# Fused two-stream attention block: interleaved layer norm, scaled copies out of PSUM, a new order of v products and weight loads, and sixteen matmuls on zeros

## The chip, the cores and the metric

The kernel runs on one core of one Trainium2 chip. A core has five engines that run their own instruction queues and meet through semaphores: PE (TensorE, matrix products, with weight loads that the profile counts apart as PEld), DVE (VectorE), ACT (ScalarE), POOL (GpSimd) and SP (SyncE, used here to issue DMAs). The metric is the device time of one execution in microseconds, lower is better. Three executions of the kernel before took 125.85, 125.17 and 124.64 us; the median is 125.17 us.

## The reference

There are two token streams, image (B = 2, 256 tokens each) and text (2 x 32 tokens), of width D = 1152, all in bfloat16. Each is normalized, scaled and shifted by rows that depend on a conditioning vector `c`, projected to q, k, v with its own weights; attention runs over the 288 joined tokens; the result goes through an output projection, is gated and added to the input.

```python
mod_i = (_silu(c) @ wmod_img).reshape(B, 6, 1, D)     # shi, sci, gai = rows 0, 1, 2
mod_t = (_silu(c) @ wmod_txt).reshape(B, 6, 1, D)     # sht, sct, gat = rows 0, 1, 2
hi = _layernorm(x_img) * (1 + sci) + shi
ht = _layernorm(x_txt) * (1 + sct) + sht
qkvi = hi @ wqkv_img
qkvt = ht @ wqkv_txt
...
scores = jnp.einsum('bqd,bkd->bqk', q, k) * D ** (-0.5)
a = jnp.einsum('bqk,bkd->bqd', softmax(scores), v)
out_i = x_img + gai * (ai @ wo_img)
out_t = x_txt + gat * (at @ wo_txt)
```

## The kernel before, in words

The order of each engine's work is the order in which the program is written (`manual_schedule`, line 62); no planner moves anything. Each engine has one ordered list of instructions; a wait stands in that list, with what follows it behind.

**Tiles.** The 512 image tokens are four tiles of 128 tokens (0 and 1 of batch 0, 2 and 3 of batch 1). The width is nine blocks of 128 (index `kt`), in four chunks of 2, 2, 2 and 3 blocks (`KC`, line 49). Normalized tokens `xn_i` are transposed on PE into `hT_i`, block by block, with the width on the partitions. Scale and shift are applied to `hT_i` after the transposes, as a factor and an addend for each partition (`apply_mod`, line 181: engine code 0 is DVE, 1 is POOL, 2 is ACT).

**Loads.** All weights are loaded by SP in one order. At the start: tiles 0 and 1 of x, then the first chunks of the scale weights `w_sc_i` and of the v weights `w_v_i`, then tiles 2 and 3 of x, then the other three pairs of chunks (lines 94 to 100), x of the text, the shift weights `w_sh_i` and the q weights `w_q_i`. The full weight matrices live in a pool of six buffers (line 54), so the seventh and later loads (lines 315 to 324) wait until the last reader of an earlier one is done: they are, in order, the text shift and scale weights `w_sh_t` and `w_sc_t`, then `w_k_i`, `w_q_t`, `w_k_t`, `w_ga_i`, `w_v_t`, `w_o_i`, `w_ga_t`, `w_o_t`. The eleventh, `w_v_t`, takes the buffer of the fifth.

**Front part (lines 214 to 269).** `silu_c` transposes `c` on PE and computes silu on ACT and DVE. Then, for each tile: `ln_stats` (three `bn_stats`, one aggregate on DVE, a square root on ACT), `ln_apply` (a reciprocal and one `tensor_scalar` on DVE), `x_transposes` (nine PE transposes into two PSUM tiles, and two ACT copies of five and four blocks into `hT_i`). `mod_scale(ch)` makes the factors of one chunk from `w_sc_i` with 18 or 27 matmuls of two columns. `v_part(i, half, ch)` adds one chunk's products to the v of tile i, half a row of 512 columns; seven such accumulators stay in PSUM until the last chunk. The statements of the four tiles are interleaved by hand.

**Middle.** `v_rest` (columns 1024 to 1151 of v), the eighth v product (line 303), the shift factors (`mod_cols` of `w_sh_i`, line 308; copies on DVE and ACT, lines 309 and 310), the shift added to `hT_i`, and `mod_rows(w_v_i, 4)`, which makes the effect of the shift on v as a row. A row made by `mod_rows` reaches the tokens by way of DRAM: PE products, a copy out of PSUM, two small DMAs from POOL to the scratch `mod_scratch` (line 344), and DMAs from POOL that read it back spread over the partitions (lines 350, 392, 533).

**q and k (line 369).** `qk_img` runs 81 matmuls of 512 columns for q, then 81 for k: first three output blocks together, then six groups of one block, nine matmuls each. `hooks` are functions called ahead of the group with that index. In the q pass, `v_shift` (DVE adds) stands ahead of group 5 and `txt_rows_shift` ahead of group 6; `txt_rows_scale` follows the q pass and also issues the four read-backs `mb_t`. In the k pass, `txt_modulate` (two DVE operations on the text tokens `xn_t`, lines 400 and 401) stands ahead of group 5, and `txt_transposes` (nine PE transposes, one ACT copy to `hT_t`, lines 406 and 407) ahead of group 8. The q and k products of the text (line 418, 162 matmuls) come next and read `hT_t`.

**Rest.** Scores and softmax, the v of the text, attention (line 500), output projections (line 568) with gates, and the output DMAs.

Of the kernel before, what the change touches and what calls it, by code (L numbers as in the profile page):

```python
# [14 lines left out]
def kernel(  # L15
# [14 lines left out]
    nc = tc.nc  # L30
# [42 lines left out]
    def load_w(src, c0, ksplits=((0, KT),)):  # L73
        t = wpool.tile([P, KT, D], bf, tag="w")
        for (k0, k1) in ksplits:
            nc.sync.dma_start(t[:, k0:k1, :], w_view(src)[:, k0:k1, c0:c0 + D])
        return t
# [31 lines left out]
    make_identity(nc, ident[:])  # L109
    eps_t = const.tile([P, 1], f32)  # L110
    nc.vector.memset(eps_t[:], EPS)
    sT32 = const.tile([P, KT, 32], bf)
    nc.gpsimd.memset(sT32[:], 0.0)
    shT32 = const.tile([P, KT, 32], bf)
    nc.gpsimd.memset(shT32[:], 0.0)


    e18 = small.tile([P, B * KT], f32, bufs=1)
    sT = const.tile([P, KT, B], bf)

    def silu_c():
        cT_ps = ps_sm.tile([P, B * KT], bf, tag="sm")
        nc.tensor.transpose(cT_ps[:], c18[:], ident[0:B * KT, 0:B * KT])
        nc.scalar.activation(e18[:], cT_ps[:], ACT.Exp, scale=-1.0)
        nc.vector.tensor_scalar_add(e18[:], e18[:], 1.0)
        nc.vector.reciprocal(e18[:], e18[:])
        nc.vector.tensor_mul(sT[:], cT_ps[:].rearrange("p (b kt) -> p kt b", b=B),
                             e18[:].rearrange("p (b kt) -> p kt b", b=B))
        nc.gpsimd.tensor_copy(sT32[:, :, 0:B], sT[:])
# [3 lines left out]
    def evac(out_ap, in_ap):  # L133
        if evac_idx[0] % 2 == 0:
            nc.vector.tensor_copy(out_ap, in_ap)  # L135
        else:
            nc.scalar.copy(out_ap, in_ap)  # L137
        evac_idx[0] += 1

    def ln_stats(x_ap, np_):  # L140
        stats = small.tile([P, NCH, 6], f32, tag="stats")
        for k in range(NCH):
            nc.vector.bn_stats(stats[0:np_, k, :], x_ap[:, k * CH:(k + 1) * CH])  # L143
        mv = small.tile([P, 2], f32, tag="mv")
        nc.vector.bn_aggr(mv[0:np_, :], stats[0:np_, :, :])
        rstd = small.tile([P, 1], f32, tag="rstd")
        nc.scalar.activation(rstd[0:np_, :], mv[0:np_, 1:2], ACT.Sqrt, bias=eps_t[0:np_, :])
        return mv, rstd

    def ln_apply(x_ap, np_, out_ap, mv, rstd):  # L150
        nc.vector.reciprocal(rstd[0:np_, :], rstd[0:np_, :])
        nc.vector.tensor_scalar(out_ap, x_ap, mv[0:np_, 0:1], rstd[0:np_, :], op0=ALU.subtract, op1=ALU.mult)  # L152

    xn_i = act.tile([P, NIT, D], bf, tag="A")
    hT_i = act.tile([P, KT, B * NI], bf, tag="Bt")

    def x_transposes(i):
        for (k0, k1) in ((0, 5), (5, KT)):
            tp = ps_mm.tile([P, 5, P], bf, tag="mm")
            for kt in range(k0, k1):  # L160
                nc.tensor.transpose(tp[:, kt - k0, :], xn_i[:, i, kt * P:(kt + 1) * P], ident[:])  # L161
            nc.scalar.copy(hT_i[:, k0:k1, i * P:(i + 1) * P], tp[:, 0:k1 - k0, :])  # L162

    mod_i = const.tile([P, 2 * KT, B], f32, name="mod_img")

    def mod_cols(wt, out_ps, j0, j1):
        for j in range(j0, j1):
# [13 lines left out]
    def apply_mod(kt, t0, t1, shift, eng):  # L181
        b = t0 // TPB
        sl = hT_i[:, kt, t0 * P:t1 * P]
        ap = mod_i[:, kt, b:b + 1] if shift else mod_i[:, KT + kt, b:b + 1]
        op = ALU.add if shift else ALU.mult
        if eng == 0:
            nc.vector.tensor_scalar(sl, sl, ap, None, op0=op)  # L187
        elif eng == 1:
            if shift:
                nc.gpsimd.tensor_scalar(sl, sl, 1.0, ap, op0=ALU.mult, op1=ALU.add)  # L190
            else:
                nc.gpsimd.tensor_scalar(sl, sl, ap, 0.0, op0=ALU.mult, op1=ALU.add)  # L192
        elif shift:
            nc.scalar.activation(sl, sl, ACT.Identity, bias=ap, scale=1.0)
        else:
            nc.scalar.activation(sl, sl, ACT.Identity, scale=ap)
# [5 lines left out]
    def v_part(i, half, ch):  # L202
        k0, k1 = KC[ch]
        if ch == 0:
            vacc[i, half] = ps_mm.tile([P, VW], f32, tag="mm", name=f"va{i}{half}")
        ps = vacc[i, half]
        for kt in range(k0, k1):
            nc.tensor.matmul(ps[:], lhsT=hT_i[:, kt, i * P:(i + 1) * P], rhs=w_v_i[:, kt, half * VW:(half + 1) * VW],  # L208
                             start=(kt == 0), stop=(kt == KT - 1))
        if k1 == KT:  # L210
            evac(v_i[:, i, half * VW:(half + 1) * VW], ps[:])


    silu_c()
    st = ln_stats(x_i[:, 0, :], P)
    ln_apply(x_i[:, 0, :], P, xn_i[:, 0, :], *st)
    x_transposes(0)
    st = ln_stats(x_i[:, 1, :], P)
    mod_scale(0, "act")
    ln_apply(x_i[:, 1, :], P, xn_i[:, 1, :], *st)  # L220
    for kt in range(*KC[0]):
        apply_mod(kt, 0, 1, False, 1)
    x_transposes(1)
    for half in range(2):
        v_part(0, half, 0)
    st = ln_stats(x_i[:, 2, :], P)
    for kt in range(*KC[0]):
        apply_mod(kt, 1, 2, False, 1)
    ln_apply(x_i[:, 2, :], P, xn_i[:, 2, :], *st)
    mod_scale(1, "act")  # L230
    for half in range(2):
        v_part(1, half, 0)
    for kt in range(*KC[1]):
        apply_mod(kt, 0, 2, False, 1)
    x_transposes(2)
    st = ln_stats(x_i[:, 3, :], P)
    for kt in range(*KC[0]):
        apply_mod(kt, 2, 3, False, 1)
    ln_apply(x_i[:, 3, :], P, xn_i[:, 3, :], *st)
    for i in range(2):  # L240
        for half in range(2):
            v_part(i, half, 1)
    x_transposes(3)
    for half in range(2):
        v_part(2, half, 0)
    for kt in range(*KC[0]):
        apply_mod(kt, 3, 4, False, 1)
    for kt in range(*KC[1]):
        apply_mod(kt, 2, 4, False, 0)
    mod_scale(2, "dve")  # L250
    for n, kt in enumerate(range(*KC[2])):
        apply_mod(kt, 0, 2, False, n % 2)
        apply_mod(kt, 2, 4, False, (n + 1) % 2)
    v_part(3, 0, 0)
    for half in range(2):
        v_part(2, half, 1)
    v_part(3, 0, 1)
    v_i = act.tile([P, NIT, D], bf, tag="A")
    SEVEN = [(i, half) for i in range(NIT) for half in range(2)][:7]
    for (i, half) in SEVEN[:4]:  # L260
# [9 lines left out]


    xn_t = act.tile([NTT, D], bf)
    st_t = ln_stats(x_t[:, :], NTT)
    ln_apply(x_t[:, :], NTT, xn_t[:, :], *st_t)
    junk = small.tile([P, 1], f32, bufs=1)
    nc.scalar.activation(junk[:], eps_t[:], ACT.Exp)
# [15 lines left out]
    def v_rest(i0, i1):  # L292
        ps = ps_mm.tile([P, NIT, P], f32, tag="mm")
        for i in range(i0, i1):
            for kt in range(KT):
                nc.tensor.matmul(ps[:, i - i0, :], lhsT=hT_i[:, kt, i * P:(i + 1) * P], rhs=w_v_i[:, kt, NM:D],  # L296
                                 start=(kt == 0), stop=(kt == KT - 1))
        evac(v_i[:, i0:i1, NM:D], ps[:, 0:i1 - i0, :])
# [3 lines left out]
    for kt in range(KT):  # L302
        nc.tensor.matmul(ps[:], lhsT=hT_i[:, kt, 3 * P:4 * P], rhs=w_v_i[:, kt, VW:NM], start=(kt == 0), stop=(kt == KT - 1))  # L303
    evac(v_i[:, 3, VW:NM], ps[:])


    mps = ps_sm.tile([P, KT, B], f32, tag="sm")
# [1 line left out]
    nc.vector.tensor_copy(mod_i[:, 0:KT, :], mps[:])  # L309
    nc.scalar.copy(shT32[:, :, 0:B], mps[:])  # L310
    for kt in range(KT):
        apply_mod(kt, 0, TPB, True, (0, 1, 2, 0, 2, 1, 0, 0, 2)[kt])
    v_rest(TPB, NIT)

    w_sh_t = load_w(wmod_txt, 0)
    w_sc_t = load_w(wmod_txt, D)
    w_k_i = load_w(wqkv_img, D, K3)
    w_q_t = load_w(wqkv_txt, 0)
    w_k_t = load_w(wqkv_txt, D)
    w_ga_i = load_w(wmod_img, 2 * D)  # L320
# [22 lines left out]
        for b in range(B):  # L343
            nc.gpsimd.dma_start(gsc[si, b, :].rearrange("(g j) -> g j", g=NGG), g_sb[b:P:32, :])  # L344

    for kt in range(KT):
        apply_mod(kt, TPB, NIT, True, (0, 1, 2, 0, 2, 1, 0, 0, 2)[kt])
    mod_rows(w_v_i, 4, lhs=shT32)
    for b in range(B):
        nc.gpsimd.dma_start(bvb[:, b, :], gsc[4, b, :].partition_broadcast(P))  # L350
# [18 lines left out]
    def qk_img(wq, blk, hooks):  # L369

        groups = [(0, 3)] + [(j, j + 1) for j in range(3, KT)]
        for (j0, j1) in groups:
            if j0 in hooks:
                hooks[j0]()
            pss = [ps_mm.tile([P, B * NI], f32, tag="mm", name="qkps") for _ in range(j0, j1)]
            for kt in range(KT):
                for j in range(j0, j1):
                    nc.tensor.matmul(pss[j - j0][:], lhsT=wq[:, kt, j * P:(j + 1) * P], rhs=hT_i[:, kt, :],  # L378
                                     start=(kt == 0), stop=(kt == KT - 1))
            for j in range(j0, j1):  # L380
                qk_evac(qkT[:, blk * KT + j, :, 0:NI], pss[j - j0][:].rearrange("p (b n) -> p b n", b=B), blk)
# [3 lines left out]
    def txt_rows_shift():  # L385
        mod_rows(w_sh_t, 0)
# [4 lines left out]
            for b in range(B):  # L391
                nc.gpsimd.dma_start(mb_t[b * NT:(b + 1) * NT, k, :], gsc[k, b, :].partition_broadcast(NT))

    qk_img(w_q_i, 0, hooks={5: v_shift, 6: txt_rows_shift})
    txt_rows_scale()

    hT_t = act.tile([P, KT, NTT], bf)

    def txt_modulate():
        nc.vector.tensor_mul(xn_t[:], xn_t[:], mb_t[:, 1, :])  # L400
        nc.vector.tensor_add(xn_t[:], xn_t[:], mb_t[:, 0, :])
# [4 lines left out]
            nc.tensor.transpose(tpt[:, kt, :], xn_t[:, kt * P:(kt + 1) * P], ident[0:NTT, 0:NTT])  # L406
        nc.scalar.copy(hT_t[:], tpt[:])

    qk_img(w_k_i, 1, hooks={5: txt_modulate, 8: txt_transposes})

    FG = 6
    for blk, wq in enumerate([w_q_t, w_k_t]):
# [222 lines left out]
```

## Time and profile before

| what | us |
|---|---|
| median of three executions (lowest, highest) | 125.17 (124.64, 125.85) |
| span of the profiled execution | 124.3 |
| PE busy | 110.7 (89%) |
| DVE busy | 55.5 (45%) |
| ACT busy | 31.6 (25%) |
| POOL busy | 21.2 (17%) |

The span is the time from the first to the last instruction of one profiled execution; the 125.17 us are the median of three executions. All instants below are microseconds from the start of that span. "Busy" counts an engine's executing instructions, and matmul ends are modelled, so PE's 89% is the share in which some matmul was under way, not its share of peak.

By stage, in that execution: the c transpose starts at 2.97, the transposes of tiles 0 to 3 at 6.96, 10.00, 14.82 and 17.84; the v products of the four chunks run from 10.93 to 30.1; the shift factors from 32.9 to 35.0; q from 37.3 to 56.2; k from 57.4 to 75.5; the text q and k products from 75.5 to 80.9; scores from 80.9; attention from 92.4; output projections from 98.9. The last load, `w_o_t`, is issued at 81.95 and lands 24.3 us later.

### The profile page before, as it was taken

What the parts mean: (1) busy time and instruction counts of PE and PEld (TensorE: products, weight loads), DVE (VectorE), ACT (ScalarE), POOL (GpSimd) and SP (SyncE); (2) the same over time, 40 slices, a digit from 0 to 9 for tenths busy, and PEclk for the clock granted to TensorE, in tenths of its full rate; (3) what the DMA queues carried; (4) which work ended last, traced back from release to release, by engine and by line L of the source; (5) the groups of instructions that cost most, each with busy time, mean ns of one, the idle gap of its engine ahead of it and who ended that gap; (6) DMA issues with size and microseconds to landing.
All of it is one profiled execution on the core that took longest, in us unless ns stands there. A gap on an engine that the chain in (4) does not pass through costs nothing.

```text
span 124.3 us, 2647 instructions
## 1 busy us (share of the span) xinstructions
PE 110.7 (89%) x1126; PEld 65.8 (53%) x1134; DVE 55.5 (45%) x131; ACT 31.6 (25%) x72; POOL 21.2 (17%) x53
## 2 busy tenths in 40 slices
PE   0057999999999999999999999899999999999980
PEld 0044554546684444445444448777656555657650
DVE  0778624146862120923022621134445656636680
ACT  4544052133572211110031121133524500012000
POOL 4005225160055030302430000002151000000000
PEclk9999999999999999999999999999999999999999
DMA  4999999999999999999999999999999997120231
GB/s 107 267 348 376 377 383 350 348 414 413 408 406 413 397 414 422 406 406 412 404 383 402 381 409 411 407 411 405 411 405 417 371 411 299 61 95 0 100 96 49
DMA packets 22728, 41.63 MB, mean 335 GB/s; under 512 B 1148, under 2 KB 6428, under 8 KB 22716
## 3 DMA queue, kind: packets, MB, share of 16 engines
q1 hardware_dynamic: 21776, 39.74, 85.1%
q0 software_dynamic: 768, 1.64, 3.4%
q8 instruction: 9, 0.15, 0.4%
q10 hardware_dynamic: 171, 0.08, 0.2%
q14 instruction: 4, 0.02, 0.0%
HBM read 40.11 MB, written 1.35 MB: 333 GB/s over the span
## 4 chain that ended last, share of the span: by engine, by line
PE 85%; DVE 6%; ACT 4%; DMA 2%; issue 2%
PE qkps L378 28%; PE ps L568 13%; PE va L208 10%; PE gps L334 5%; PE ps L418 4%; PE aps L500 4%; PE sps L438 4%; PE mps L169 3%; ACT hT_i L162 2%; PE tp L161 2%; PE ps L587 2%; DMA c<-in_c_dram 2%; PE ps L515 2%; PE ps L296 2%; PE ps L303 2%
## 5 line engine op out<-in xcount | busy, mean ns | idle before, releaser
L378 PE MATMUL qkps<-hT_i,t 128*128 128x512 bf16 x157 | 35.4, 379 | 0.3
L378 PEld LDWEIGHTS <-t 128*128 128x128 bf16 x162 | 15.5, 98 | 18.9 <-issue 0.7
L568 PE MATMUL ps<-t,aT 128*128 128x384 bf16 (+2 forms) x117 | 18.1, 314 | 0.0
L208 PE MATMUL va<-w_v_i,hT_i 128*128 128x512 bf16 x60 | 16.0, 408 | 0.5 <-issue 0.2
L568 PEld LDWEIGHTS <-aT 128*128 128x128 bf16 x117 | 10.9, 98 | 6.8 <-issue 0.5
L571 DVE SCALAR_TENSOR_TENSOR tmp<-ps,rs,gb 128x384 bf16<-128x384 f32 (+2 forms) x13 | 7.6, 586 | 6.9 <-PE ps L568 6.9
L344 POOL DMA_DIRECT2D mod_scratch<-g_sb x8 | 4.8, 596 | 34.3 <-DVE g_sb L135 22.5
L208 PEld LDWEIGHTS <-hT_i 128*128 128x128 bf16 x63 | 6.2, 103 | 6.9 <-issue 1.5
L161 PE MATMUL tp<-ident,xn_i 128*128 128x128 bf16 x36 | 4.1, 287 | 5.4 <-DVE xn_i L152 5.4
L192 POOL TENSOR_SCALAR hT_i<-hT_i,mod_img 128x128 bf16<-128x128 bf16 (+1 forms) x14 | 6.1, 449 | 15.0 <-ACT mod_img L179 6.2
L362 DVE TENSOR_SCALAR qkT<-qkps 128x512 bf16<-128x512 f32 x5 | 3.4, 687 | 9.1 <-PE qkps L378 9.1
L137 ACT CAST qkT<-qkps 128x512 bf16<-128x512 f32 x5 | 2.8, 586 | 16.0 <-PE qkps L378 16.0
L161 PEld LDWEIGHTS <-xn_i 128*128 128x128 bf16 x36 | 3.3, 133 | 6.6 <-DVE xn_i L152 6.1
L135 DVE CAST qkT<-qkps 128x512 bf16<-128x512 f32 x4 | 2.8, 688 | 8.3 <-PE qkps L378 8.3
L162 ACT COPY hT_i<-tp 128x640 bf16<-128x640 bf16 (+1 forms) x8 | 4.7, 642 | 6.7 <-PE tp L161 6.7
L143 DVE BATCH_NORM_STATS2 stats<-x_i 128x6 f32<-128x384 bf16 x12 | 5.9, 546 | 0.0
L500 PE MATMUL aps<-pT,v_i 128*128 128x288 bf16 x36 | 5.4, 287 | 0.3 <-ACT pT L489 0.3
L418 PE MATMUL ps<-hT_t,t 128*128 128x64 bf16 x162 | 5.0, 193 | 0.5 <-issue 0.5
L418 PEld LDWEIGHTS <-t 128*128 128x128 bf16 x162 | 4.9, 98 | 0.9 <-issue 0.6
L364 ACT ACTIVATE qkT<-qkps 128x512 bf16<-128x512 f32 x4 | 2.3, 596 | 11.5 <-PE qkps L378 11.5
L334 PE MATMUL gps<-t,sT 128*32 128x288 bf16 x144 | 5.1, 287 | 0.0
L187 DVE TENSOR_SCALAR hT_i<-hT_i,mod_img 128x256 bf16<-128x256 bf16 x14 | 4.3, 368 | 1.5 <-ACT hT_i L162 1.3
(108 smaller groups left out, 119.0 us busy)
## 6 DMA issues: line engine op xcount, KB each, us to landing
t<-in_wmod_txt_dram SPq DMA_DIRECT2D x3, 2592.0 KB, 24.2
t<-in_wqkv_txt_dram SPq DMA_DIRECT2D x3, 2592.0 KB, 20.8
t<-in_wmod_img_dram SPq DMA_DIRECT2D x2, 2592.0 KB, 18.7
t<-in_wqkv_img_dram SPq DMA_DIRECT2D x6, 864.0 KB, 15.8
t<-in_wo_img_dram SPq DMA_DIRECT2D x1, 2592.0 KB, 22.1
t<-in_wo_txt_dram SPq DMA_DIRECT2D x1, 2592.0 KB, 24.3
w_sc_i<-in_wmod_img_dram SPq DMA_DIRECT2D x3, 576.0 KB, 7.8
w_v_i<-in_wqkv_img_dram SPq DMA_DIRECT2D x3, 576.0 KB, 7.9
```

What stands on the lines that cost most here:

```text
L143: nc.vector.bn_stats(stats[0:np_, k, :], x_ap[:, k * CH:(k + 1) * CH])
L161: nc.tensor.transpose(tp[:, kt - k0, :], xn_i[:, i, kt * P:(kt + 1) * P], ident[:])
L162: nc.scalar.copy(hT_i[:, k0:k1, i * P:(i + 1) * P], tp[:, 0:k1 - k0, :])
L192: nc.gpsimd.tensor_scalar(sl, sl, ap, 0.0, op0=ALU.mult, op1=ALU.add)
L208: nc.tensor.matmul(ps[:], lhsT=hT_i[:, kt, i * P:(i + 1) * P], rhs=w_v_i[:, kt, half * VW:(half + 1) * VW], start=(kt == 0), stop=(kt == K ...
L334: nc.tensor.matmul(gps[32 * g:32 * g + 32, :], lhsT=lhs[:, kt, :], rhs=w_blk[:, kt, g * VC:(g + 1) * VC], start=(kt == 0), stop=(kt == KT ...
L378: nc.tensor.matmul(pss[j - j0][:], lhsT=wq[:, kt, j * P:(j + 1) * P], rhs=hT_i[:, kt, :], start=(kt == 0), stop=(kt == KT - 1))
L418: nc.tensor.matmul(ps[:, j - j0, :], lhsT=wq[:, kt, j * P:(j + 1) * P], rhs=hT_t[:, kt, :], start=(kt == 0), stop=(kt == KT - 1))
L438: nc.tensor.matmul(sps[:], lhsT=qkT[:, ft, b, q0:q0 + P], rhs=qkT[:, KT + ft, b, :], start=(ft == 0), stop=(ft == KT - 1))
L500: nc.tensor.matmul(aps[:], lhsT=v_i[:, b * TPB + kj, dt * P:(dt + 1) * P], rhs=pTs[b][:, kj, :], start=(kj == 0), stop=False)
L568: nc.tensor.matmul(ps[:, 0:cw], lhsT=aT[:, dt, t0:t0 + P], rhs=w_o_i[:, dt, cs], start=(dt == 0), stop=(dt == KT - 1))
L571: nc.vector.scalar_tensor_tensor(tmp[:, 0:cw], ps[:, 0:cw], rsum[(b, qi)][:], gb[:, b, cs], op0=ALU.mult, op1=ALU.mult)
```

## The change

- `ln_stats` is split: the first of the three `bn_stats` of the next tile is issued ahead of the reciprocal and `tensor_scalar` of the tile before it (`ln_next`, `ln_out`), on the same engine, DVE.
- `x_transposes` only transposes. The first two blocks of tiles 0 to 2, and the first four of tile 3, leave PSUM by ACT activations that multiply by the factor (`evac_scaled`); the other blocks leave by plain ACT copies (`evac_plain`). The separate POOL multiplications of chunk 0, and for tile 3 the DVE ones of chunk 1, go. Those of chunk 2 are all on DVE for batch 0 and all on POOL for batch 1, where they alternated.
- `wz`, a 128 x 512 tile of zeros, is written by DVE, and `warm(n)` issues n matmuls of 512 columns on it into PSUM tiles that nothing reads: 4 ahead of the c transpose, 7 ahead of the transposes of tile 0, 3 behind them, 2 ahead of the transposes of tile 1.
- The v products are in another order: chunk 1 of tiles 0 and 1 comes behind the transposes of tile 3.
- `v_rest(TPB, NIT)` moves ahead of the shift factors; the shift is added to both batches in one loop ahead of `mod_rows(w_v_i, 4)`.
- `w_k_i` is loaded ahead of `w_sh_t` and `w_sc_t`, so the fifth buffer holds `w_k_i`, and `w_v_t` waits for that one.
- The shift and scale rows of the text move to the k pass, ahead of group 3; `txt_modulate` and `txt_transposes` move behind the k pass.

```diff
+    wz = const.tile([P, VW], bf)
+    nc.vector.memset(wz[:], 0.0)
...
+    def warm(n):
+        for _ in range(n):
+            ps = ps_mm.tile([P, VW], f32, tag="mm", name="wps")
+            nc.tensor.matmul(ps[:], lhsT=wz[:, 0:P], rhs=wz[:], start=True, stop=True)
...
-    def ln_stats(x_ap, np_):
-        stats = small.tile([P, NCH, 6], f32, tag="stats")
-        for k in range(NCH):
+    def ln_stats(x_ap, np_, k0, k1, stats=None):
+        if stats is None:
+            stats = small.tile([P, NCH, 6], f32, tag="stats")
+        for k in range(k0, k1):
             nc.vector.bn_stats(stats[0:np_, k, :], x_ap[:, k * CH:(k + 1) * CH])
+        return stats
+
+    def ln_std(stats, np_):
         mv = small.tile([P, 2], f32, tag="mv")
...
     def x_transposes(i):
+        tps = []
         for (k0, k1) in ((0, 5), (5, KT)):
...
-            nc.scalar.copy(hT_i[:, k0:k1, i * P:(i + 1) * P], tp[:, 0:k1 - k0, :])
+            tps.append(tp)
+        return tps
+
+    def evac_scaled(i, tps, n):
+        for kt in range(n):
+            nc.scalar.activation(hT_i[:, kt, i * P:(i + 1) * P], tps[0][:, kt, :], ACT.Identity,
+                                 scale=mod_i[:, KT + kt, i // TPB:i // TPB + 1])
+
+    def evac_plain(i, tps, n):
+        nc.scalar.copy(hT_i[:, n:5, i * P:(i + 1) * P], tps[0][:, n:5, :])
+        nc.scalar.copy(hT_i[:, 5:KT, i * P:(i + 1) * P], tps[1][:, 0:KT - 5, :])
...
+    warm(4)
     silu_c()
...
+    def ln_next(i, first):
+        if first:
+            lns[i] = ln_stats(x_i[:, i, :], P, 0, 1)
+        else:
+            ln_stats(x_i[:, i, :], P, 1, NCH, lns[i])
+            lns[i] = ln_std(lns[i], P)
+
+    def ln_out(i):
+        ln_apply(x_i[:, i, :], P, xn_i[:, i, :], *lns[i])
+
+    ln_next(0, True)
+    ln_next(0, False)
+    ln_next(1, True)
+    ln_out(0)
+    warm(7)
+    tps = x_transposes(0)
+    evac_plain(0, tps, 2)
+    ln_next(1, False)
+    ln_next(2, True)
+    ln_out(1)
+    warm(3)
     mod_scale(0, "act")
...
+    evac_scaled(0, tps, 2)
+    warm(2)
+    tps = x_transposes(1)
+    evac_scaled(1, tps, 2)
+    ln_next(2, False)
+    ln_next(3, True)
+    ln_out(2)
+    evac_plain(1, tps, 2)
+    for i in range(2):
+        for half in range(2):
+            v_part(i, half, 0)
+    tps = x_transposes(2)
+    evac_scaled(2, tps, 2)
+    ln_next(3, False)
+    ln_out(3)
     mod_scale(1, "act")
...
+    evac_plain(2, tps, 2)
     for kt in range(*KC[1]):
         apply_mod(kt, 0, 2, False, 1)
...
+    for kt in range(*KC[1]):
+        apply_mod(kt, 2, 3, False, 0)
+    v_part(2, 0, 0)
+    tps = x_transposes(3)
+    evac_scaled(3, tps, 4)
+    evac_plain(3, tps, 4)
     for i in range(2):
         for half in range(2):
             v_part(i, half, 1)
...
+    v_part(2, 0, 1)
     mod_scale(2, "dve")
...
+    for kt in range(*KC[2]):
+        apply_mod(kt, 0, 2, False, 0)
+        apply_mod(kt, 2, 4, False, 1)
+    for (i, half) in ((2, 1), (3, 0)):
+        for ch in range(2):
+            v_part(i, half, ch)
...
     evac(v_i[:, 3, VW:NM], ps[:])
+    v_rest(TPB, NIT)
...
     for kt in range(KT):
-        apply_mod(kt, 0, TPB, True, (0, 1, 2, 0, 2, 1, 0, 0, 2)[kt])
-    v_rest(TPB, NIT)
-
+        apply_mod(kt, 0, TPB, True, (0, 1, 2, 0, 2, 0, 1, 0, 2)[kt])
+        apply_mod(kt, TPB, NIT, True, (2, 0, 1, 0, 2, 0, 0, 1, 2)[kt])
+
+    w_k_i = load_w(wqkv_img, D, K3)
     w_sh_t = load_w(wmod_txt, 0)
     w_sc_t = load_w(wmod_txt, D)
-    w_k_i = load_w(wqkv_img, D, K3)
...
-    for kt in range(KT):
-        apply_mod(kt, TPB, NIT, True, (0, 1, 2, 0, 2, 1, 0, 0, 2)[kt])
...
-    qk_img(w_q_i, 0, hooks={5: v_shift, 6: txt_rows_shift})
-    txt_rows_scale()
+    qk_img(w_q_i, 0, hooks={5: v_shift})
...
+    def txt_rows():
+        txt_rows_shift()
+        txt_rows_scale()
+
+    qk_img(w_k_i, 1, hooks={3: txt_rows})
+    txt_modulate()
+    txt_transposes()
```

More of the change, by code (lines that the diff above doesn't have):

```diff
@@ L155 @@
     hT_i = act.tile([P, KT, B * NI], bf, tag="Bt")
+    mod_i = const.tile([P, 2 * KT, B], f32, name="mod_img")
     def x_transposes(i):
+        tps = []
         for (k0, k1) in ((0, 5), (5, KT)):
@@ L161, in x_transposes @@
                 nc.tensor.transpose(tp[:, kt - k0, :], xn_i[:, i, kt * P:(kt + 1) * P], ident[:])
-            nc.scalar.copy(hT_i[:, k0:k1, i * P:(i + 1) * P], tp[:, 0:k1 - k0, :])
-    mod_i = const.tile([P, 2 * KT, B], f32, name="mod_img")
+            tps.append(tp)
[7 more added lines that the diff above has]
+        nc.scalar.copy(hT_i[:, 5:KT, i * P:(i + 1) * P], tps[1][:, 0:KT - 5, :])
     def mod_cols(wt, out_ps, j0, j1):
@@ L211, in v_part @@
             evac(v_i[:, i, half * VW:(half + 1) * VW], ps[:])
+    warm(4)
     silu_c()
[L215 to L218, printed above, removed]
-    mod_scale(0, "act")
[L220 to L229, printed above, removed]
+    lns = {}
+    def ln_next(i, first):
[17 more added lines that the diff above has]
+    warm(3)
+    mod_scale(0, "act")
+    evac_scaled(0, tps, 2)
[13 more added lines that the diff above has]
+    ln_out(3)
     mod_scale(1, "act")
-    for half in range(2):
-        v_part(1, half, 0)
+    evac_plain(2, tps, 2)
     for kt in range(*KC[1]):
         apply_mod(kt, 0, 2, False, 1)
[L235 to L239, printed above, removed]
+    for kt in range(*KC[1]):
[4 more added lines that the diff above has]
+    evac_plain(3, tps, 4)
     for i in range(2):
@@ L242 @@
             v_part(i, half, 1)
[L243 to L249, printed above, removed]
-    mod_scale(2, "dve")
[L251 to L257, printed above, removed]
+    v_part(2, 0, 1)
+    mod_scale(2, "dve")
+    for kt in range(*KC[2]):
[4 more added lines that the diff above has]
+            v_part(i, half, ch)
     v_i = act.tile([P, NIT, D], bf, tag="A")
@@ L272 @@
     xn_t = act.tile([NTT, D], bf)
-    st_t = ln_stats(x_t[:, :], NTT)
+    st_t = ln_std(ln_stats(x_t[:, :], NTT, 0, NCH), NTT)
     ln_apply(x_t[:, :], NTT, xn_t[:, :], *st_t)
@@ L407, in txt_transposes @@
         nc.scalar.copy(hT_t[:], tpt[:])
-    qk_img(w_k_i, 1, hooks={5: txt_modulate, 8: txt_transposes})
+    def txt_rows():
[4 more added lines that the diff above has]
+    txt_transposes()
     FG = 6
```

## The prediction

> **What bounds the kernel now.** I read the page's slices and chain first, to see which engine sets the end.
>
> ```profile
> PE   0057999999999999999999999899999999999980
> PEclk9999999999999999999999999999999999999999
> PE 85%; DVE 6%; ACT 4%; DMA 2%; issue 2%
> ```
>
> A slice is 3.1 us. From the fourth on PE is full until the last. So the time is the start of PE's dense part plus PE's work behind it, and a change pays only if dense work starts earlier and no hole opens later. I take PE's timeline for the early part.
>
> ```profile
> 10.93 1.91 PE L208 MATMUL va<-w_v_i,hT_i 128*128 128x512 bf16 x4
> 15.77 1.89 PE L208 MATMUL va<-w_v_i,hT_i 128*128 128x512 bf16 x8
> 17.84 0.68 PE L161 MATMUL tp<-ident,xn_i 128*128 128x128 bf16 x9 [0.18 <-DVE xn_i L152]
> ```
>
> Four products took as long as eight did 5 us later. With the longest and the usual duration of one (0.634 and 0.379 us by line 208's own view), the pitch is (1.91-0.63)/3 = 0.427 us at first and (1.89-0.38)/7 = 0.216 us later, though the granted clock reads 1.00 throughout. Nine transposes at 14.82 took 1.11 us and here 0.68.
>
> Then, what fed those transposes, from the timeline of DVE and of ACT.
>
> ```profile
> 9.32 0.62 DVE L152 TENSOR_SCALAR xn_i<-x_i,mv,rstd 128x1152 bf16<-128x1152 bf16 x1
> 9.94 1.48 DVE L143 BATCH_NORM_STATS2 stats<-x_i 128x6 f32<-128x384 bf16 x3
> ...
> 15.60 1.18 ACT L162 COPY hT_i<-tp 128x640 bf16<-128x640 bf16 x2 [2.09 <-PE tp L161]
> 16.66 0.31 ACT L147 ACTIVATE rstd<-mv,eps_t 128x1 f32<-128x1 f32 x1
> ```
>
> Tile 1 was normalized by 9.94 and the statistics of tile 2 came behind it. Tile 2 itself, issued at 3.34, has this in its view:
>
> ```profile
> DMA to landing us min/median/max: 6.6/6.6/6.6
> ```
>
> So it landed at 9.94. Tile 3's square root waited behind ACT copies until 16.66. Last, the text rows' way, in the timeline from 56 to 81 and the chain of the same stretch.
>
> ```profile
> 57.47 0.46 DVE L338 TENSOR_SCALAR g_sb<-gps 128x288 bf16<-128x288 f32 x1 [0.54 <-PE gps L334]
> 58.21 1.10 POOL L344 DMA_DIRECT2D mod_scratch<-g_sb  x2 [6.06 <-DVE g_sb L338]
> 63.69 0.98 POOL L392 DMA_DIRECT2D mb_t<-mod_scratch  x2 [3.35 <-DMA mod_scratch<-g_sb]
> 69.34 0.75 DVE L400 TENSOR_TENSOR xn_t<-xn_t,mb_t 64x1152 bf16<-64x1152 bf16 x1 [3.33 <-DMA mb_t<-mod_scratch]
> 70.13 0.75 DVE L401 TENSOR_TENSOR xn_t<-xn_t,mb_t 64x1152 bf16<-64x1152 bf16 x1
> ```
>
> ```profile
> 56.20 1.22 PE gps L334 x36
> 57.41 0.75 PE qkps L378 x3
> ...
> 75.47 4.35 PE ps L418 x149
> ```
>
> The scale rows leave PE at 57.41 and are back on the text tokens' partitions at 69.34, 11.93 us later. All 81 k products lay beside that, so PE never waited.
>
> **The front part.** Durations are those of the profiled execution.
>
> *Zeros.* PE is busy 0.23 us of the first 7. `wz` costs DVE between 0.06 (memset of one column, line 111) and 0.33 us (288 columns on POOL, line 113), so PE starts at about 1.0 to 1.2 and four products at 0.427 are issued by 2.9; c landed at 2.93 (0.75+2.18). Seven more end their pitch near 6.1, before tile 0 is ready. The five others stand before the wait for tile 1 below. The sixteen cost nothing while that idle time lasts; without it, 16 x 0.216 to 0.427 = 3.5 to 6.8 us. What they may bring is the 0.216 pitch before 11 us. In this trace it came after about 5.9 us of nearly unbroken work (10.0 to 15.9); from 1.1 the same length ends at 7.0, so I take tile 1's work at 0.216, and price the other case as a rival.
>
> [...]
>
> *Layer norm.* `bn_stats` go at 0.49 each (1.47/3); filling the square root's gap (0.36) with one of them delays tile 0 by 0.15, to 7.1. But the first one of tile 2 now stands ahead of tile 1's reciprocal on DVE. DVE reaches it near 8.3 and tile 2 lands at 9.94. So tile 1, behind it, is normalized at 9.94+0.49+0.75 = 11.2 instead of 9.94: a new wait of 1.6 us, with everything of DVE queued behind it. From there DVE runs without gaps: two more statistics and aggregate 1.25, one statistic of tile 3 0.49, tile 2's output 0.75 (13.7), 1.25 (14.95), a root 0.35, tile 3's output 0.75: 16.05, against 17.78 before. The root of tile 3 fits because ACT now has two scaled blocks (0.25 each, from the 0.258 of a 128-column ACT copy) ahead of it, not two long copies.
>
> *PE.* Tile 1's transposes 11.3 to 11.85 (pitch 0.056), eight products to 13.6, tile 2's transposes at 13.75, the second factor at 14.3 to 14.8, two products, tile 3's transposes at 16.05. Their second half needs the PSUM tile that ACT empties at about 16.4 (copies of 0.45 and 0.59 from 15.4), and POOL's two factors of chunk 1 (0.47 each from 15.4) end at 16.35. Dense work begins at 16.75 with 53 products and two factor steps left: 53 x 0.216 + 0.50 + 0.75 = 12.7, so the v products end at 29.4. Before, they ended at 30.08: PE was later (17.84) but had 47 products left. The gain is **0.7**. The last chunk of `w_v_i`, issued at 12.05 and landing 10.2 later, is there.
>
> *Shift.* Before, `v_rest` (1.03) lay between the shift factors (end 35.04) and `mod_rows`, and covered the two copies that end at 35.52. Now nothing covers them: PE waits 0.53. The additions need not end: by DVE's 0.30, ACT's 0.46 and POOL's 0.54 pitch each block of `hT_i` is ready before the q pass, which takes 3 x 0.216 per block, reaches it. So the q pass starts 0.7-0.53 = **0.17 earlier**, at 37.1.
>
> **The text rows.** Before, 38.19 us passed from the start of q (37.28) to the text products (75.47). Now: q 17.5, the first k group 5.82, both rows 2.44, small issue gaps 0.2: the rows end 25.95 after q's start, and only six groups, 54 x 0.216 = 11.65, are left beside the way by DRAM. That way is unchanged in kind: 11.93, two DVE operations 0.79+0.75, hand-over 0.05, transposes to ACT's start 0.47, copy 0.64, hand-over 0.05 = 14.68. So the text products start 40.63 after q's start, **2.44 later** than before in relation to q; PE has a hole of about 3 us with only nine transposes in it. Both rows first pass POOL's queue of scratch writes, but the shift rows are out 1.2 earlier and their writes end before the scale's begin, so the scale's last read-back comes as before.
>
> The nearest rows for the price are the eight scratch writes (4.4 to 5.5 us to land) and the four `mb_t` reads (4.8 to 5.2); the lower bound is a DMA with idle engines, c at 2.18. I keep 4.6 and 5.0, because the DMA share is 1.04 in this stretch and the loads of that time are still queued. With 2.18 twice the way is 5.3 shorter and the hole is gone.
>
> [...]
>
> **Loads.** `w_k_i` and the two text matrices swap places; together they are the same bytes, so the last lands as before near 57.8 (41.94 + 15.8), needed at 61.7. `w_v_t` now waits until k ends, about 74.8, with `w_o_i`, `w_ga_t`, `w_o_t` behind it on SP; before it was issued at 61.94. `w_ga_i` fills the queues to 78.4 (55.26+23.1), so the stream goes on, and the later three have 6 to 7 us in hand before their readers. [...]
>
> **Sum.** -0.7 + 0.53 + 2.44 = **+2.3 us**: the span goes from 124.3 to 126.6, and the time, which stands 0.9 above the span in the median, from 125.17 to about **127.4**.
>
> **Rivals.**
> - *The front gains more.* If tile 2 lands before DVE asks (8.3), tile 3 is ready at 14.8, 1.25 earlier: 126.2. Against it: 9.94 is measured, and nothing ahead of that load changes. 13%.
> - *No hole, not slower.* The two trips through DRAM take 2.6 us less together, because SP holds `w_v_t` back and the queues thin out. It decides from about 1.3 less per trip on. Then -0.7+0.53 is left, and the transposes' 0.36 stay as they were: 125.0; with the gain of the first rival 123.7. Against it: `w_ga_i` is still in flight. 13%, 4% of it with both.
> - *The zeros do not raise the pitch*, or the 2 us of waiting at 9.2 to 11.3 lowers it again. Eight products and two sets of transposes cost 8 x 0.211 + 18 x 0.05 = 2.6 more, of which about 2.0 reach tile 3's root behind ACT's copies: 129.4. 12%. A lowered pitch in the 3 us hole would cost the same kind of sum.
> - *Forecast*: 62%, own range 126.4 to 128.4 by a DMA trip of 4.4 or 5.5 and half a microsecond either way in the front.
>
> **How the numbers follow.** 1% of 125.17 is 1.25 us, about what a measurement here can tell from no change. Slower by more: the forecast but for 3% at its low end, and the cold case, 70%. Within: the first rival, 9% of the second, and that 3%, 25%. Faster: 5%, both gains together and what I have not thought of. The range 125.5 to 129.3 holds the forecast, the first rival and the near half of the cold case; it leaves out the second and the far half, under 20%.
>
> **What would show it.** In the changed profile: the first `bn_stats` of tile 2 waiting on the load of x until about 9.9 with tile 1's reciprocal behind it; v products at 0.216 from 11.9; PE waiting 0.5 us between the shift factors and the v row; DVE waiting for `mb_t` past the end of k and PE idle near 75 to 77.5. I am wrong if the text products follow k within a microsecond, or if the v products end before 28.5 or after 30.5.

## The result, and the profile after

| | before | changed |
|---|---|---|
| median (lowest, highest), us | 125.17 (124.64, 125.85) | 129.03 (128.59, 130.49) |
| span of the profiled execution | 124.3 | 126.5 |

The ratio is 1.0322, with a 95% interval of 1.0254 to 1.0389: the change makes the kernel 3.2% slower. The spans differ by 2.2 us, where the prediction had 2.3; the medians differ by 3.9. So there are two things to explain. Ratios here and below leave out executions more than 1.5% above the fastest of the same kernel, while medians count all of them.

First the page, in the lines shown of before: slices of 3.2 us with the busy share of PE and the granted clock in tenths, and the shares of the chain that ended last ("issue" is time in which an engine waited for nothing that the profile shows, a q marks an engine's instruction queue).

```profile
PE   6977889999989999999999965899999999999990
PEclk9999999999999999999999999999999999999999
PE 70%; DMA 13%; DVE 8%; issue 3%; SPq 2%; ACT 2%; POOL 1%; DVEq 0%; ACTq 0%
```

PE has work from the first slice on (the zeros), and a dent in the 24th and 25th, at 73 to 79 us, where before had none. DMA, 2% of the chain before, is 13%. The timeline of PE has the early part (start, duration, then the group):

```profile
11.47 0.68 PE L175 MATMUL tp<-ident,xn_i 128*128 128x128 bf16 x9 [0.69 <-DVE xn_i L163]
11.99 1.89 PE L231 MATMUL va<-w_v_i,hT_i 128*128 128x512 bf16 x8
16.30 0.68 PE L175 MATMUL tp<-ident,xn_i 128*128 128x128 bf16 x9 [0.93 <-DVE xn_i L163]
16.82 2.32 PE L231 MATMUL va<-w_v_i,hT_i 128*128 128x512 bf16 x10
```

Eight v products in 1.89 from 11.99 on, and nine transposes in 0.68: the fast pitch of 0.216 us stands 4 us earlier than before. Tile 3's transposes start at 16.30 (before 17.84). DVE's timeline shows what tile 1 waited for, the chain what came between v and q, and then the text rows' way:

```profile
10.18 0.56 DVE L151 BATCH_NORM_STATS2 stats<-x_i 128x6 f32<-128x384 bf16 x1 [2.00 <-DMA x_i<-in_x_img_dram]
10.65 0.15 DVE L162 RECIPROCAL rstd<-rstd 128x1 f32<-128x1 f32 x1
```

```profile
33.50 2.03 PE mps L192 x81
...
35.83 0.18 ACT shT L352
36.01 0.04 issue
36.05 1.29 PE gps L376 x36
37.34 23.42 PE qkps L418 x108
60.76 1.24 PE gps L376 x36
...
62.71 4.42 DMA mod_scratch<-g_sb
...
69.33 5.56 DMA mb_t<-mod_scratch
...
76.57 0.45 PE tpt L445 x9
77.02 0.02 issue
77.04 0.65 ACT hT_t L446
77.69 0.04 issue
77.73 3.98 PE ps L463 x131
```

Tile 1's reciprocal stood 2.0 us behind tile 2's load. PE waited from 35.53 to 36.05 for the copy of the shift factors; before, `v_rest` lay there, and the chain stayed on PE:

```profile
33.03 2.02 PE mps L169 x81
35.04 1.03 PE ps L296 x18
36.07 1.22 PE gps L334 x36
37.28 0.32 PE qkps L378
```

And PE, done with k at 74.84, began the text products at 77.73: the chain leaves PE for the two trips through DRAM.

### The profile page after: what moved, and what is told of

Its sections match the earlier page's. It is cut to its first block, busy times and chain, and to the rows that moved or that the text cites. A ratio compares the mean times of both kernels' runs of the same rounds, so it can differ in the third digit from the quotient of the medians.

```text
span 126.5 us, 2691 instructions
## 1 busy us (share of the span) xinstructions
PE 115.7 (91%) x1150; PEld 66.6 (53%) x1150; DVE 55.6 (44%) x132; ACT 33.6 (27%) x82; POOL 18.2 (14%) x45
## 4 chain that ended last, share of the span: by engine, by line
PE 70%; DMA 13%; DVE 8%; issue 3%; SPq 2%; ACT 2%; POOL 1%; DVEq 0%; ACTq 0%
PE qkps L418 19%; PE ps L613 13%; PE va L231 9%; DMA x_i<-in_x_img_dram 5%; DMA mb_t<-mod_scratch 4%; PE ps L463 4%; PE gps L376 4%; PE aps L545 4%; PE sps L483 4%; DMA mod_scratch<-g_sb 3%; PE mps L192 2%; DVE stats L151 2%; PE ps L632 2%; PE ps L560 2%; PE ps L337 2%
## 5 line engine op out<-in xcount | busy, mean ns | idle before, releaser
L231 PE MATMUL va<-w_v_i,hT_i 128*128 128x512 bf16 x63 | 14.4, 379 | 0.0
L142 DVE CAST qkT<-qkps 128x512 bf16<-128x512 f32 x5 | 3.4, 690 | 14.0 <-PE qkps L418 14.0
L123 PE MATMUL wps<-wz 128*128 128x512 bf16 x16 | 7.6, 626 | 1.2 <-DVE wz L113 1.2
L404 ACT ACTIVATE qkT<-qkps 128x512 bf16<-128x512 f32 x5 | 2.9, 596 | 14.3 <-PE qkps L418 14.3
L144 ACT CAST qkT<-qkps 128x512 bf16<-128x512 f32 x4 | 2.3, 586 | 16.3 <-PE qkps L418 16.3
L215 POOL TENSOR_SCALAR hT_i<-hT_i,mod_img 128x256 bf16<-128x256 bf16 x6 | 3.1, 529 | 17.4 <-ACT mod_img L202 10.9
L402 DVE TENSOR_SCALAR qkT<-qkps 128x512 bf16<-128x512 f32 x4 | 2.7, 688 | 6.1 <-PE qkps L418 6.1
L175 PE MATMUL tp<-ident,xn_i 128*128 128x128 bf16 x36 | 3.2, 243 | 2.3 <-DVE xn_i L163 2.3
L175 PEld LDWEIGHTS <-xn_i 128*128 128x128 bf16 x36 | 2.4, 109 | 4.8 <-DVE xn_i L163 4.8
L142 DVE CAST aT<-aps 128x288 bf16<-128x288 f32 x9 | 3.7, 454 | 2.6 <-PE aps L551 2.6
```

The source lines that it names most:

```text
L123: nc.tensor.matmul(ps[:], lhsT=wz[:, 0:P], rhs=wz[:], start=True, stop=True)
```

## The experiments

All times of one row below were taken beside the kernel before on the same chip; "tile 3 out" is tile 3's normalized output counted from the landing of tile 2's load, since that landing alone moved between 9.35 and 10.44 from execution to execution (not given for the last row, where that load was moved).

| run | profiled span | v end to q start | q start to text products | tile 3 out | median | ratio to before (95%) |
|---|---|---|---|---|---|---|
| before again | 123.8 | 7.5 | 38.1 | 7.9 | 125.60 | 1.0015 (0.9987-1.0044) |
| changed | 126.5 | 8.1 | 40.5 | 6.1 | 129.03 | 1.0322 (1.0254-1.0389) |
| changed again | 128.4 | 8.1 | 42.0 | 6.1 | 130.27 | 1.0412 (1.0367-1.0458) |
| text stage back | 122.5 | 8.1 | 38.1 | 6.1 | 126.36 | 1.0005 (0.9958-1.0052) |
| hole filled with zeros | 126.5 | 8.1 | 41.9 | 6.1 | 128.69 | 1.0214 (1.0147-1.0281) |
| no zeros | 130.9 | 9.2 | 41.4 | 8.1 | 131.48 | 1.0487 (1.0434-1.0540) |
| tile 1 first | 127.2 | 8.1 | 40.4 | 5.4 | 128.18 | 1.0227 (1.0174-1.0281) |
| shift covered | 125.5 | 7.5 | 40.4 | 6.1 | 127.73 | 1.0184 (1.0141-1.0227) |
| before + 11 zeros | 123.2 | 7.5 | 38.1 | 7.3 | 125.34 | 0.9999 (0.9967-1.0032) |
| before + 16 zeros | 122.1 | 7.5 | 38.1 | 6.5 | 123.99 | 0.9914 (0.9894-0.9934) |
| combined | 121.9 | 7.5 | 38.1 | 5.4 | 124.22 | 0.9922 (0.9886-0.9959) |
| combined, x first | 121.3 | 7.5 | 38.1 | - | 123.30 | 0.9858 (0.9838-0.9877) |

"v end" and "q start" are the starts of the last v product of line 231 (208) and of the first q product.

A warning on the spans: from the first text product to the end they hold 48.8 to 49.1 us in most profiles, but 47.9 in "text stage back", "hole filled" and the two combined kernels, 48.3 with sixteen zeros and 49.6 without zeros, and no edit aimed at that part. Of the 1.9 us between "before again" and "combined", 1.0 lies there and 0.9 in the front.

**Before again.** The kernel before, not edited.

> The kernel before, unchanged. The changed kernel's four executions stand 2.08 to 2.19 us above their own spans (126.5 to 128.3), the profile of before only 0.87 above its span. Theory A (the profiled execution of before was a late one of its kernel, because PE's pitch of 0.216 us came as late as 15.9): spans near 123.0, time again 2.1 above them, the pitch of 0.216 reached earlier than 15.9. Theory B (what lies around the span is larger in the changed kernel): spans near 124.3, time 0.9 above.

Span 123.8, at a time of 125.62: 1.8 around it. So theory A holds for the most part: the execution whose profile the prediction read was a late one. The eight products at 0.216 started at 15.19 instead of 15.77, and c was transposed 0.33 earlier. Of before's executions on record, those with a span of 124.1 to 124.4 took 125.85 to 126.15, so the profile of 124.3 fits a time near 126 and not the median of 125.17. The changed kernel's spans stand 2.1 below their times, so 0.25 of the difference lies outside the span and stays unexplained.

**Text stage back.**

```diff
-    w_k_i = load_w(wqkv_img, D, K3)
     w_sh_t = load_w(wmod_txt, 0)
     w_sc_t = load_w(wmod_txt, D)
+    w_k_i = load_w(wqkv_img, D, K3)
...
-    qk_img(w_q_i, 0, hooks={5: v_shift})
+    qk_img(w_q_i, 0, hooks={5: v_shift, 6: txt_rows_shift})
+    txt_rows_scale()
...
-    qk_img(w_k_i, 1, hooks={3: txt_rows})
-    txt_modulate()
-    txt_transposes()
+    qk_img(w_k_i, 1, hooks={5: txt_modulate, 8: txt_transposes})
```

> The changed kernel with the text stage of before: both text rows in and behind the q pass, modulation and transposes inside the k pass, the text shift and scale weights loaded ahead of w_k_i. Theory (the hole behind k is the cost): the hole of 3 us goes, the text products follow k at once, span 126.5 - 2.4 = 124.1, time about 126.2 or lower; and the granted clock, which was 0.971 to 0.985 in three of four executions of the changed kernel, is 1.00 again. Rival (the rows cost the same wherever they stand, the front is late): span within 0.5 of 126.5.

The hole went: 38.1 us from q to the text products instead of 40.5, the 2.4 forecast. The chain of that run passes from k to the text products on PE alone:

```profile
68.27 4.05 PE qkps L418 x18
72.31 0.36 PE tpt L446 x9
72.68 2.05 PE qkps L418 x9
74.73 4.72 PE ps L462 x162
```

Its span is 4.0 below the changed kernel's profile; the rest is tile 2's load, which landed 0.8 earlier in this execution, and a gap of 0.9 within the text products that this one lacks (79.82 in before's chain, 81.71 in the changed kernel's). The traces hold a hint: in the seven profiles with that gap, a 16 KB transfer of instructions (queue q8) starts 2.3 to 2.7 us after the first text product; in the six without it, it starts 1.3 us after it or sooner, or 3.7 where the products ran at half the clock. No run tested that it is the cause.

The forecast of a clock of 1.00 failed: eight of the twelve executions had mean clocks of 0.985 or 0.986. The median, 126.36, is 1.8 above the profiled execution's 124.56 (clock 1.00) and 0.8% above before's 125.36, where the ratio reads 1.0005. So the second cost is still in this kernel.

**Hole filled with zeros.** Seven more products on zeros behind the k pass.

```diff
     qk_img(w_k_i, 1, hooks={3: txt_rows})
+    warm(7)
     txt_modulate()
```

> The changed kernel with seven more products on zeros between the k pass and the text modulation, in PE's idle time there (7 x 0.216 = 1.5 us, in a hole of 1.7 us ahead of the transposes). Theory (the idle hole lets the granted clock fall behind it in most executions): granted clock 1.00 in all executions, span near 126.5 in each, median time 128.6 or lower. Rival (the clock falls elsewhere or for another reason): clocks of 0.97 to 0.985 stay, median near 129.0.

The theory fell: four of six executions had mean clocks of 0.982 to 0.987 and stood 1.2 us or more above the fastest (127.27, clock 1.00), and in the profile the lowered stretch lay not behind the hole, but at the start of the q pass, 36.77 to 40.19. The zeros themselves did no harm: the transposes started at 77.40, when DVE had done its second operation (76.59 + 0.75).

**Changed again**, on another chip.

> The changed kernel, unchanged, for more executions beside the others. If the lowered clock behind the shift stage is what parts its executions, most of them lie 0.5 to 2 us above the fastest, which is near 128.5 (126.5 and 2.1 around it); a profile with a mean clock under 1 has its lowered stretch of 3.41 us at 36 to 41. If the hole behind k lowers it, the stretch lies at 78 to 85.

Same place, and all six executions had mean clocks of 0.974 or 0.987. No execution of before on record, in any of the runs, was under 0.993 (one stretch of 3.41 us at a half is 0.5 x 3.41 of some 123 us, 0.014 off the mean). The windows view (from:to, length, busy time of PE, PEld, DVE, ACT, POOL with counts of all instructions that touch the window, granted clock, DMA share, GB/s):

```profile
34.20:37.60 3.40, 2.87 (x101) 2.43 (x99) 1.72 (x7) 1.87 (x7) 1.47 (x3) 1.00 1.04 409
37.60:41.00 3.40, 3.40 (x13) 1.17 (x10) 1.12 (x4) 1.08 (x3) 2.04 (x4) 0.50 1.05 409
41.00:44.40 3.40, 3.40 (x17) 1.55 (x16) 0.00 (x0) 0.00 (x0) 0.00 (x0) 1.00 1.04 403
```

In the stretch at 0.50, 8 q products started (the other matmuls counted there had begun before it), in the next one 16, and the q pass with k up to the text products took 42.0 instead of 40.5. That is 1.5 us for this lowered stretch; half of 3.41, 1.7, would be lost if PE did nothing else in it than matmuls at half the pace. The stretch ahead holds some 70% of the 81 shift matmuls of two columns, the 0.5 us of waiting, and the v row's 32-column products.

**Shift covered.** The last `v_rest` back between the shift factors and the v row.

```diff
     evac(v_i[:, 3, VW:NM], ps[:])
-    v_rest(TPB, NIT)
...
     for kt in range(KT):
-        apply_mod(kt, 0, TPB, True, (0, 1, 2, 0, 2, 0, 1, 0, 2)[kt])
-        apply_mod(kt, TPB, NIT, True, (2, 0, 1, 0, 2, 0, 0, 1, 2)[kt])
+        apply_mod(kt, 0, TPB, True, (0, 1, 2, 0, 2, 1, 0, 0, 2)[kt])
+    v_rest(TPB, NIT)
+    for kt in range(KT):
+        apply_mod(kt, TPB, NIT, True, (0, 1, 2, 0, 2, 1, 0, 0, 2)[kt])
```

> The changed kernel with the two last v_rest products and the shift additions in the order of before: v_rest between the shift factors and the v row. In two runs the clock was granted at a half for 3.41 us just behind that place (36.8 to 40.2), where PE had 81 matmuls of two columns and then waited 0.5. Theory A (that place lowers the clock): granted clock 1.00 or only one lowered window behind the hole near 78 to 85, span 126.0, median near 128.0. Theory B (the hole behind k lowers it): clocks of 0.97 to 0.985 as before, median near 128.5, only the 0.53 of waiting gone.

Theory A: v end to q start fell from 8.1 to 7.5, with the 0.53 of waiting in it; no lowered stretch in the profile; four of six executions at a clock of 1.00 (the changed kernel: one of ten). The hole is still in this kernel. The other pair says the same: with neither hole nor cover (text stage back), 8 of 12 executions had a mean clock of 0.985 or 0.986; with cover and no hole (combined, below, which also has tile 1 first), 3 of 11. So the cover removes most of the lowered stretches and not all; where the others lay is not known, since each execution has its mean clock on record but only the profiled one its stretches.

**No zeros.** `warm` issues nothing.

```diff
-        for _ in range(n):
+        for _ in range(0):
```

> The changed kernel without its sixteen products on zeros (the tile is still written). Theory (they bring the 0.216 pitch ahead of tile 1 and cost nothing themselves): eight v products at 0.427 and two sets of transposes at 0.107 again, tile 3's transposes about 2 us later than 16.3, span 128.5. Rival (tile 1 waits for x and DVE sets the pace, so the pitch does not matter): span within 0.5 of 126.5.

The theory's direction holds: tile 3's transposes at 17.71 against 16.30 (2.0 later counted from tile 2's landing, as expected) and the ratio 1.0487 against 1.0322. Of the 4.4 us between the profiled spans, 1.4 is there; v end to q start takes 1.1 longer, q to the text products 0.9 and those products 0.8, and this execution had two lowered stretches. The first begins at 37.30, at the shift stage again; the second does follow the hole:

```profile
78.30:81.70 3.40, 0.81 (x22) 0.78 (x23) 1.50 (x2) 0.82 (x2) 0.00 (x0) 1.00 1.04 411
81.70:85.10 3.40, 3.40 (x70) 3.40 (x67) 0.56 (x1) 0.00 (x0) 0.00 (x0) 0.50 1.06 416
```

PE busy 0.81 of 3.4, then a stretch at a half. So this execution had a stretch at half the clock at each place.

**Tile 1 first.**

```diff
-    ln_next(2, True)
     ln_out(1)
+    ln_next(2, True)
```

> The changed kernel with one line moved: tile 1's reciprocal and output ahead of the first statistics of tile 2, so they don't wait for tile 2's load (10.15). Theory: tile 1's transposes at about 9.7 instead of 11.47, and since the statistics of tile 2 still start at 10.15 but then run together, tiles 2 and 3 come 0.6 earlier: span 0.6 lower than the changed kernel's in an execution with the same clock record (126.5 with none lowered). Rival (the wait for x is hidden, because tile 2's load sets the pace in both orders): no difference.

Tile 1's transposes came at 9.55, and tile 3 was out 5.4 after tile 2's landing instead of 6.1: the 0.6 was 0.7. The profiled span does not show it (127.2), because the clock was at 0.50 from 15.0 to 18.4, behind a stretch with PE busy 1.91 of 3.4 (its wait for tile 2 lay there):

```profile
11.60:15.00 3.40, 1.91 (x31) 1.14 (x29) 2.90 (x10) 2.48 (x9) 0.24 (x1) 1.00 1.10 379
15.00:18.40 3.40, 2.80 (x14) 1.70 (x15) 1.09 (x3) 2.29 (x8) 0.88 (x2) 0.50 1.09 385
```

The gain in the chain is shown. For its worth in time there are three executions at a clock of 1.00, with spans of 125.3 to 125.7, against the one of the changed kernel, 126.5; the landing of tile 2's load, which moves by up to a microsecond between executions, is mixed into this difference.

**Zeros in the kernel before.** Eleven, then all sixteen, with nothing else of the change (the lines that make `wz` and `warm` are not shown; the last two added lines stand in the run with sixteen alone).

```diff
...
+    warm(4)
     silu_c()
...
+    warm(7)
     x_transposes(0)
     st = ln_stats(x_i[:, 1, :], P)
+    warm(3)
     mod_scale(0, "act")
+    warm(2)
```

> The kernel before with zeros alone: four products ahead of the transpose of c and seven ahead of tile 0's transposes. Theory (the late pitch delays tile 2's transposes, and so ACT's copies and tile 3's root): pitch 0.216 by 11, tile 3's transposes 1.7 earlier, span 122.1, time 1.3% to 1.5% below before. Rival (loads or DVE set the pace of the front): within 0.5 of 123.8.

> The kernel before with all sixteen products on zeros, in the places of the changed kernel: eleven ahead of tile 0's transposes, three behind them and two behind the first factors. With eleven, the clock had risen at 6.3 and was lowered again from 9.73 to 13.15, where PE idled. Theory (zeros help only if they also fill the wait for tile 1): no lowered stretch before 16, tile 3's transposes at 16.0 or earlier, span 122.3, median 0.7% to 1.2% below before. Rival (the lowering comes anyway): median equal to before.

Eleven gain nothing (0.9999), sixteen gain 0.9%. The windows, first of eleven, then of sixteen:

```profile
6.30:9.70 3.40, 1.14 (x28) 1.02 (x27) 2.93 (x8) 1.50 (x4) 0.57 (x2) 1.00 1.04 369
9.70:13.10 3.40, 3.23 (x32) 2.10 (x33) 2.77 (x8) 1.37 (x3) 1.06 (x3) 0.50 1.06 349
```

```profile
5.80:9.20 3.40, 2.51 (x34) 1.36 (x32) 2.57 (x8) 1.80 (x5) 0.06 (x1) 1.00 0.95 330
9.20:12.70 3.50, 2.01 (x31) 1.25 (x31) 3.05 (x8) 1.48 (x3) 1.58 (x4) 1.00 1.09 376
```

The five later zeros make the difference between 1.14 and 2.51 us of busy PE, and the clock stays; no lowered stretch followed in any of the six executions with sixteen, where the mean is 0.993 or more. Tile 3's transposes came at 16.66 and 16.32 (before again 17.41). With sixteen, the v products ended at 28.55, 1.0 earlier than in the changed kernel, where tile 2's load landed 0.3 later: in these two profiles the other edits of the front brought no gain.

**Combined.** The changed front with tile 1 first, and the shift and text stages of before: the diffs of "text stage back", "shift covered" and "tile 1 first" together.

> The changed kernel's front with tile 1's output ahead of the statistics of tile 2, and with the shift stage and the text stage of before. Theory: 122.5 (the run with the text stage of before) less 0.5 for the covered copies less 0.6 for tile 1: span 121.4, no lowered clock behind the shift stage, median near 123.5, 1.3% to 1.5% below before. Rival (the front's gain is bound by loads): span 122.3 or more.

Span 121.9, median 124.22: faster than before by 0.8%, not by 1.3%. Tile 3's output stands 5.4 behind a load that landed late here (10.07).

**Combined, x first.** The combined kernel with one line moved:

```diff
     load_x(1)
-    load_pair(0)
     load_x(2)
     load_x(3)
+    load_pair(0)
```

> The best version so far (the changed front with tile 1's output first, shift and text stages of before) with tiles 2 and 3 of x loaded ahead of the first chunks of weights. Theory (tile 2's load, landing between 9.4 and 10.2, sets the front): tile 2 lands near 6, tile 3 is normalized near 13.5 instead of 15.5, the v products end 1.4 earlier, where the last chunk of v weights (22.3 to 23.3) becomes the bound: span 120.5. Rival (the first weight chunks, 1.4 us later, set it instead): span 121.5 to 122.5.

Tile 2 landed at 5.8, tile 3 was out at 14.83, 0.6 earlier and not 2: DVE reached tile 2's statistics only at 9.41, so its own work is the bound now. The gain in the front is half of what I expected, but the wait for a load that moves is gone, and the four executions lie within 0.05 us of each other. This is the fastest version, 1.4% below before.

## Why the prediction was right, and where its size was off

- *Zeros at no cost.* Nearly: c was transposed at 3.05, 0.1 later than in the profile of before, but 0.4 to 0.5 later than in "before again" and "no zeros" (2.64 and 2.54), and tile 0 followed 0.4 later (7.03 against 6.64 and 6.65). Their gain was in the forecast only as the pitch from tile 1 on. That held by a narrow margin: the clock record has the full clock from 10.87 on, 0.6 before tile 1's transposes. Without the zeros the changed kernel stood 4.9% above before instead of 3.2% (4.1% on the other chip), and alone they are worth 0.9%.
- *Tile 1 behind tile 2's load.* 1.6 forecast, 2.0 measured; one moved line took 0.7 out of the chain.
- *Dense work from 16.75, v products until 29.4.* Measured 16.82 and 29.55. But the gain of 0.7 was counted from a late profile of before: it is 0.5 against that one (30.08) and 0.1 against "before again" (29.65). So it is partly luck that the spans differ by 2.2 where 2.3 was forecast; against "before again" they differ by 2.7.
- *0.53 of waiting in the shift stage.* 0.52. What I did not see is a stretch at half the clock behind it: the profiles of "changed again" (37.62 to 41.03, a loss of 1.5 us) and "hole filled" (36.77 to 40.19) have one there, and nine of the changed kernel's ten executions had mean clocks of 0.971 to 0.987. I put a price on a lowered pitch only in front of tile 1 and in the hole.
- *Text products 40.63 after q's start.* Measured 77.73 - 37.34 = 40.39 in the chain, 2.2 later than before; by the table's starts 40.5 against 38.1, 2.4 later. The trips took 4.4 and 5.6 us, against the 4.6 and 5.0 of the nearest rows. The 2.18 us of c, at the start of the span, were no measure: no transfer to or from `mod_scratch` in the profiles of before and changed landed in under 4.4.
- *Loads, with no term in the sum.* No product waited for a weight.
- *Span 126.6.* Measured 126.5.
- *Time 0.9 above the span.* This term was the one far off, and carries 1.2 of the 1.6 us between 127.4 and 129.03: an execution's time stands 1.8 (before) to 2.1 (changed) above its own span, and I had set one execution's span against another's median. The remaining 0.4 is the median span of the changed kernel's four executions, 126.95: three of them had mean clocks of 0.971 to 0.985, the profiled one 1.00.

The rival that denied the hole fell. The first rival's premise, tile 2 landing before DVE asks at 8.3, came in no profile with that order of loads (9.35 to 10.44). The third, a lowered clock, is true beside the forecast, in the changed kernel's profiles behind the shift stage, which I had not named; the two places that I had named had it once each, the hole in "no zeros" and the wait in the front in "tile 1 first".

## What to carry to other kernels

Before moving a row that travels through DRAM, add up the whole way to its last reader (in the changed kernel 14.7 us, from 63.01, where PE goes on with k behind both rows, to the text products at 77.73, with trips of 4.4 and 5.6 beside a DMA share of 1.04 and 1.05) and compare it with the independent products that remain behind its new place. In an engine's queue, work for the next tile that fills a gap of 0.36 us must not wait for that tile's load (2.0 us here). And the thin matmul stretch of some 3 us in the shift stage cost twice in some executions: once as time, with 0.5 us of waiting in it, and again where 3.41 us at half the clock followed over dense products (1.5 us in "changed again"). So put dense work in between: with it, four of six executions had a clock of 1.00, without it one of ten. Last, before setting a profile's span against a median, ask for the time of that same execution.

## What the runs showed of the hardware

The clock records of the trace (start and end of a stretch at full or half clock, in us from the start of the span; records of the last few us are left out):

```
hole filled       full 6.05-36.77    half 36.77-40.19   full 40.19-125.5
changed again     full 6.90-37.62    half 37.62-41.03   full 41.03-129.8
before + 11       full 6.32-9.73     half 9.73-13.15    full 13.15-122.4
tile 1 first      full 4.78-15.02    half 15.02-18.43   full 18.43-127.7
no zeros          full 16.82-37.30   half 37.30-40.72   full 40.72-81.68   half 81.68-85.09   full 85.09-132.9
before            full 15.74-125.0
changed           full 10.87-126.9
```

In these records every half stretch between full ones lasts 3.41 or 3.42 us, and the full ones that end in a half stretch last 3.41, 10.24, 20.48, 30.72 (twice) and 40.96 us: 1, 3, 6, 9 and 12 times 3.413. The first full stretch starts at another instant in each execution, between 4.78 and 16.82. Stretches of 3.4 us with PE busy 2.87 (changed again) and 1.91 us (tile 1 first) came before a half stretch, while 2.01 and 2.51 (before + 16 zeros) did not, and neither did 2.86 in the changed kernel's own profile:

```profile
34.80:38.20 3.40, 2.86 (x70) 1.96 (x67) 2.61 (x10) 2.37 (x7) 2.15 (x4) 1.00 1.04 412
38.20:41.60 3.40, 3.40 (x17) 1.52 (x16) 0.23 (x1) 0.20 (x1) 1.36 (x2) 1.00 1.04 404
```

So busy time alone does not settle it, and what lowers the clock stays open. This execution has the same wait in the shift stage as "changed again", 0.5 us. Steps of 3.413 us counted on from the start of its full stretch, 10.87, have one that begins at 34.8, and in "changed again", from 6.90, at 34.2; the one from 34.8 has q products at its end. That whether a half stretch follows depends on where these steps fall would fit this; it is my estimate, and no run tested it.

With the zeros the first full stretch began earlier: at 4.78 to 10.87 us in the five listed profiles that have them, at 15.74 and 16.82 in the two without. The records begin only with that stretch, which is why the mean clock of before reads 1.00 though its v products from 10.93 on went at 0.427.
